# One table of moments for four engines, and a 16-bit split for the transposes

## The chip, the cores and the metric

The kernel runs on one core of one Trainium2 chip. The metric is the device time of one execution in microseconds (us), lower is better. In this text PE is the matrix engine (TensorE), DVE the vector engine, ACT the scalar engine (activations), POOL is GpSimd, and SP is the queue that issues all transfers. A trace of one execution is read through its views: the page, the stretches, the groups by line, the timeline of an engine, the waits.

## The reference, cut to what matters

```python
# q, k, v: (8 batches, 8 heads, 576 positions, 64)
scores = q @ k.T / sqrt(64)
mask = (rel >= 0) & (rel < 64)              # each query sees itself and the 63 keys before it
attn = softmax(where(mask, scores, -1e9))
x = (attn @ v) as (4608 tokens, 512)        # heads side by side
h = x @ w_in                                # w_in: (512, 2048), w_out: (2048, 512)
g = maximum(h, 0) + log1p(exp(-abs(h)))     # softplus
out = g @ w_out                             # (4608, 512)
```

## The kernel before

The 4608 tokens are cut into 12 blocks of 384 (`TB`). The attention of a block is done in four *pairs* of heads (128 of the 512 columns each), so there are 48 pairs. The FFN of a block has 16 *steps*, one for each 128 of the 2048 inner columns, so there are 192 steps.

A pair goes through stages. SP loads q, k and v. PE makes the scores (L216, 12 products, which the trace counts as 24 matmuls). DVE adds the mask and takes the row's extreme (L224, six times). ACT takes the exponential and its row sums (L235). DVE normalises (L243 to L245). The 384x128 attention weights have to be turned over. In the first two blocks (`by_pe`) PE does that (L253) and ACT copies both halves of the result to `pt` (L254). In the ten others the weights are scaled, ACT rounds them to 16 bits (L264, tile `nat`), DVE takes the rounded part away for a second 16-bit tile (L267), SP's transposing transfer turns both (L261, `tr`), and DVE adds them into `pt` (L271). Then PE multiplies with v (L285, called AV here), ACT rounds the result to the matrix engine's format (L290, first part of `x`), and DVE takes the remainder (L291, second part).

A step is an *up* group of 12 matmuls into one bank `ps_h` (L307), the softplus (ACT L311 to L313, DVE L315), the rounding of g and its remainder (L317 on ACT or DVE, L318 on DVE), and a *down* group of nine matmuls into three banks `ps_o` (L328). Weights, x and g are each held as a rounded part plus a remainder, and a product takes three matmuls. `ps_h` has two banks, g three buffers.

The weights come as 64-bit words in 16 *tiles*, one for each inner step (`load_w`). A tile is a 1 MB load, one ACT pass (L162), three DVE passes (L163 to L165), two rounding copies on ACT (L168) and two remainders on DVE (L169). Step f of any block needs tile f, so in the order of steps (four of block 0, sixteen of block 1, the other twelve of block 0, then block 2 and on) the twentieth step, which is number 19 when counted from 0, is the first to use tile 15. Steps are counted from 0 below.

The order of PE's instructions is the one in which the code is written out: `events` gives each stage a number by hand (`CONVERT`, `BASE`, `STG0`, `EARLY_UP` and so on) and sorts by it, and `MANUAL` keeps PE to that. The three other engines' orders (DVE, ACT, SP) are found by the framework's scheduler, which sees the same list.

Of the kernel before, what the change touches and what calls it, by code (L numbers as in the profile page):

```python
# [11 lines left out]
FP16 = mybir.dt.float16  # L12
# [31 lines left out]
def window_attention_softplus_ffn(  # L44
# [97 lines left out]
    def load_w(f):  # L142


        if f < NE + 4:
# [11 lines left out]
        for raw, w, m0, m1 in parts:
# [3 lines left out]
            wb = w.bitcast(U32)  # L161
            nc.scalar.activation(w, high.bitcast(F32), AF.Abs, scale=REBIAS)  # L162
            nc.vector.tensor_scalar(wb, wb, 3, None, ALU.logical_shift_left)  # L163
            nc.vector.scalar_tensor_tensor(wb, high, 0x80000000, wb, ALU.bitwise_and, ALU.bitwise_or)  # L164
            nc.vector.scalar_tensor_tensor(wb, low, 29, wb, ALU.logical_shift_right, ALU.bitwise_or)  # L165
            for m in range(m0, m1):
                hi, lo = [weight(m, i, f) for i in range(2)]
                nc.scalar.copy(hi, w[:, m - m0, :])  # L168
                nc.vector.tensor_tensor(lo, w[:, m - m0, :], hi.bitcast(F32), ALU.subtract)  # L169
# [5 lines left out]
    def attention(g, hp):  # L175
# [12 lines left out]
        q_in = ld.tile([P, TB], F32, name="q_in", bufs=2)  # L188
        k_in = ld.tile([P, CH + TB], F32, name="k_in", bufs=2)
# [7 lines left out]
        v_in = att.tile([P, 2 * NJ, P], F32, name="v_in", bufs=2)  # L197
# [8 lines left out]
        if g == 0:  # L206

            st = spare(FIRST[hp], [P, 2, NJ, P], F32, "st0")
        else:
            st = att.tile([P, 2, NJ, P], F32, name="st", bufs=2)  # L210
        mn = att.tile([P, 2, NJ], F32, name="mn", bufs=2)
        sm = att.tile([P, 2 * NJ], F32, name="sm", bufs=2)
# [7 lines left out]
        for j in range(NJ):  # L220
            t = (t0 + j * P) % S
            m = mask_at[0] if t == 0 else mask_at[1] if t + P > S else mask
            for hh in range(2):
                nc.vector.tensor_tensor_reduce(  # L224
                    st[:, hh, j, :], sps[hh][:, j * P : (j + 1) * P], m,
                    QSCALE, 3.0e38, ALU.add, ALU.min, mn[:, hh, j : j + 1],
                )
            if by_pe or j == NJ - 1:
                yield

        sv = st.rearrange("p h j c -> p (h j) c")
        for hh in range(2):
# [5 lines left out]
            if not by_pe:  # L238
                yield
        if by_pe:  # L240
            nc.vector.tensor_scalar(sm, sm, 1.0e-9, None, ALU.add)
        else:
            nc.vector.tensor_scalar(sm, sm, 1.0e-9, 1.0 / P_UNIT, ALU.add, ALU.mult)  # L243
        nc.vector.reciprocal(sm, sm)
        nc.vector.tensor_tensor(sv, sv, sm.unsqueeze(2).to_broadcast([P, 2 * NJ, P]), ALU.mult)  # L245
        if by_pe:

            yield
            pt = att.tile([P, 2, TB], F32, name="pt")
            for hh in range(2):  # L250
                pp = bank()
                for j in range(NJ):
                    tp(pp[:, j * P : (j + 1) * P], sv[:, hh * NJ + j, :], ident)  # L253
                nc.scalar.copy(pt[:, hh, :], pp[:, :TB])  # L254
        else:

            nat = att.tile([P, 2, 2 * NJ, P], FP16, name="nat")
# [6 lines left out]
            nc.scalar.copy(nat[:, 0, :, :], sv)  # L264
            turn(0)
            yield
            nc.vector.tensor_tensor(nat[:, 1, :, :], sv, nat[:, 0, :, :], ALU.subtract)  # L267
# [21 lines left out]
        unit = 1.0 if by_pe else 1.0 / P_UNIT  # L289
        nc.scalar.mul(x_t[0], av[:, :TB], unit)  # L290
        nc.vector.scalar_tensor_tensor(x_t[1], av[:, :TB], unit, x_t[0].bitcast(F32), ALU.mult, ALU.subtract)  # L291
# [7 lines left out]
    def ffn_up(g, f):  # L299
        x = xs[g]  # L300
        hps = ps_h.tile([P, 512], F32, name="ps_h")
        hv = hps[:, :TB]
        fs = slice(f * P, (f + 1) * P)
# [10 lines left out]
        gf = u  # L314
        nc.vector.scalar_tensor_tensor(gf, hv, 0.0, u, ALU.max, ALU.add)  # L315
        gt = [ff.tile([P, TB], F32R, name=f"g{i}", bufs=3) for i in range(2)]
        (nc.scalar.copy if g < 2 or f % 2 else nc.vector.tensor_copy)(gt[0], gf)  # L317
        nc.vector.tensor_tensor(gt[1], gf, gt[0].bitcast(F32), ALU.subtract)  # L318
# [110 lines left out]
```

## Time and profile before

| | |
|---|---|
| median of 3 runs | 969.87 us (968.57 to 971.11) |
| the profiled execution's own time | 974.21 us |
| its span, first to last instruction | 972.4 us |
| PE busy | 923.3 us, 95% |
| DVE busy | 539.0 us, 55% |
| ACT busy | 564.5 us, 58% |
| matmuls | 6384 |
| read from and written to memory | 56.62 MB and 10.22 MB |

The busy shares are means over very different parts: a beginning in which weights are made ready, and a long even stretch. The page cuts the span into 40 slices of 24.3 us and gives a digit for each (9 is 90% busy or more). A row of a timeline gives the start, the length, the engine, the line, output and inputs, how many instructions were merged, and in brackets the idle time ahead with what ended it. The length of a DVE or ACT row reaches a little into the next one, so what an instruction costs in a full queue is the distance between two starts.

### The profile page before, as it was taken

Reading aid. Unit: us, or ns where it says so; the run is one execution under the profiler, and the core shown is the slowest. Engines: PE = TensorE matmul, PEld = TensorE weight load, DVE = VectorE, ACT = ScalarE, POOL = GpSimd, SP = SyncE. Lnnn points to the kernel's source line nnn. Section 1 sums busy time; section 2 is a strip of 40 time slices with the busy share of each in tenths; the row PEclk is TensorE's granted clock in tenths of the full one; section 3 lists DMA queues with packets and bytes.
Section 4 is the critical chain, followed back from the end, with each engine's and each line's share of the span. In section 5 each row is a group of like instructions: output and inputs, shape, how many; then the busy total and the mean of one; then the engine's idle time right before and its main releaser. Section 6 shows DMA issues by size and latency. Waiting matters only on the chain.

```text
span 972.4 us, 16615 instructions
## 1 busy us (share of the span) xinstructions
PE 923.3 (95%) x6384; PEld 814.9 (84%) x6384; DVE 539.0 (55%) x1431; ACT 564.5 (58%) x1433; POOL 3.9 (0%) x23
## 2 busy tenths in 40 slices
PE   5458989999999999999999999999999999999998
PEld 4347978888888888888888888888888888889997
DVE  4897684646546545545555554554554555553332
ACT  5666676656555655655655555565565565554443
POOL 1000000000000000000000000000000000000000
PEclk9568989999999999999999999999999999999999
DMA  7764333513334212322321321322323332210000
GB/s 223 261 219 146 131 109 52 148 51 117 65 53 104 80 51 80 93 62 69 100 67 51 117 67 52 112 64 60 93 74 68 83 85 68 65 33 2 33 1 33
DMA packets 124047, 83.65 MB, mean 86 GB/s; under 512 B 67136, under 2 KB 116032, under 8 KB 122432
## 3 DMA queue, kind: packets, MB, share of 16 engines
q1 hardware_dynamic: 123968, 82.60, 30.3%
q8 instruction: 50, 0.82, 0.4%
q14 instruction: 29, 0.24, 0.1%
HBM read 56.62 MB, written 10.22 MB: 69 GB/s over the span
## 4 chain that ended last, share of the span: by engine, by line
PE 87%; DMA 6%; DVE 3%; ACT 3%; issue 0%; SPq 0%; ACTq 0%; DVEq 0%
PE ps_h L307 41%; PE ps_o L328 39%; PE ps_a L285 4%; DMA raws<-in_w_words_dram 4%; PE ps_a L216 3%; DMA raw<-in_w_words_dram 2%; ACT st L235 1%; ACT ws L162 1%; DVE w L169 1%; DVE ws L164 0%; DVE ws L165 0%; DMA part<-raw 0%; DVE st L245 0%; ACT wh L162 0%; DVE st L224 0%
## 5 line engine op out<-in xcount | busy, mean ns | idle before, releaser
L307 PE MATMUL ps_h<-x,w 128*128 128x384 f32 x2304 | 443.8, 341 | 3.4 <-DVE u L315 3.4
L328 PE MATMUL ps_o<-w,g 128*128 128x512 f32 x1728 | 433.5, 395 | 1.4 <-DVE g L318 1.4
L307 PEld LDWEIGHTS ps_h<-x,w 128*128 128x128 f32 x2304 | 409.1, 189 | 24.1 <-issue 6.9
L328 PEld LDWEIGHTS ps_o<-w,g 128*128 128x128 f32 x1728 | 322.2, 188 | 62.3 <-DVE g L318 2.0
L315 DVE SCALAR_TENSOR_TENSOR u<-ps_h,u 128x384 f32<-128x384 f32 x192 | 107.0, 557 | 253.4 <-ACT u L313 249.7
L311 ACT ACTIVATE u<-ps_h 128x384 f32<-128x384 f32 x192 | 93.5, 487 | 226.1 <-PE ps_h L307 226.1
L235 ACT ACTIVATE st<-st,mn 128x128 f32<-128x128 f32 x288 | 111.9, 391 | 67.1 <-DVE mn L224 67.1
L318 DVE TENSOR_TENSOR g<-u,g 128x384 fp32r<-128x384 f32 x192 | 106.6, 555 | 38.7 <-ACT g L317 33.8
L312 ACT ACTIVATE u<-u 128x384 f32<-128x384 f32 x192 | 100.9, 526 | 5.8
L313 ACT ACTIVATE u<-u 128x384 f32<-128x384 f32 x192 | 100.9, 525 | 5.7
L317 ACT CAST g<-u 128x384 fp32r<-128x384 f32 x112 | 57.4, 512 | 57.7 <-DVE u L315 56.6
L285 PEld LDWEIGHTS ps_a<-pt,v_in 128*64 128x64 f32 x1104 | 40.1, 146 | 34.1 <-issue 20.2
L224 DVE CUSTOM_DVE_ANT_0 st<-ps_a,mask 128x128 f32<-128x128 f32 x276 | 61.8, 286 | 9.6 <-PE ps_a L216 9.6
L285 PE MATMUL ps_a<-pt,v_in 128*64 128x64 f32 x1104 | 47.6, 236 | 16.8 <-ACT pt L254 11.3
L235 ACT ACTIVATION_READ_ACCUMULATOR st<-st,mn 128x1 f32 x288 | 54.0, 188 | 0.0
L271 DVE TENSOR_TENSOR pt<-tr 128x768 f32<-128x768 f16 x40 | 38.3, 958 | 22.8 <-PE ps_a L285 21.2
L216 PE MATMUL ps_a<-k_in,q_in 64*64 64x128 f32 x1104 | 44.8, 297 | 3.8 <-DMA k_in<-in_kT_dram 3.8
L245 DVE TENSOR_TENSOR st<-st,sm 128x768 f32<-128x768 f32 x48 | 46.0, 958 | 1.4
L216 PEld LDWEIGHTS ps_a<-k_in,q_in 64*64 64x64 f32 x1104 | 32.7, 144 | 8.6 <-POOL mask L135 3.8
L267 DVE TENSOR_TENSOR nat<-st,nat 128x768 f16<-128x768 f32 x40 | 38.1, 952 | 1.4 <-ACT nat L264 1.4
L243 DVE TENSOR_SCALAR sm<-sm 128x6 f32<-128x6 f32 x40 | 6.9, 172 | 54.4 <-ACT st L235 54.3
L264 ACT CAST nat<-st 128x768 f16<-128x768 f32 x40 | 33.3, 832 | 0.5 <-DVE st L245 0.5
(48 smaller groups left out, 295.6 us busy)
## 6 DMA issues: line engine op xcount, KB each, us to landing
v_in<-in_v_dram SPq DMA_DIRECT2D x44, 384.0 KB, 3.6
raws<-in_w_words_dram SPq DMA_DIRECT2D x12, 1024.0 KB, 7.2
k_in<-in_kT_dram SPq DMA_DIRECT2D x44, 224.0 KB, 4.0
q_in<-in_qT_dram SPq DMA_DIRECT2D x48, 192.0 KB, 3.7
out_dram<-raw SPq DMA_DIRECT2D x12, 512.0 KB, 3.0
raw<-in_w_words_dram SPq DMA_DIRECT2D x8, 512.0 KB, 3.9
out_dram<-raw SPq DMA_DIRECT2D x12, 256.0 KB, 4.3
v_in<-in_v_dram SPq DMA_DIRECT2D x4, 320.0 KB, 4.2
```

The costliest lines, as they stand in the source:

```text
L216: mm(sps[hh][halves[u], j * P : (j + 1) * P], q_in[heads[hh], a * CH : (a + 1) * CH], k_in[heads[hh], a * CH : (a + 2) * CH], start=True, ...
L224: nc.vector.tensor_tensor_reduce(st[:, hh, j, :], sps[hh][:, j * P : (j + 1) * P], m, QSCALE, 3.0e38, ALU.add, ALU.min, mn[:, hh, j : j + 1],)
L235: nc.scalar.activation(sv[:, i, :], sv[:, i, :], AF.Exp, bias=mn[:, hh, j : j + 1], scale=-1.0, accum_out=sm[:, i : i + 1])
L285: mm(av[heads[hh], cs], v_in[:, a, heads[hh]], pt[:, hh, cs], start=(a == 0), stop=(a == 2 * NJ - 1), skip_group_check=True,)
L307: mm(hv, weight(0, a, f)[:, c * P : (c + 1) * P], x[b][c], start=(i_mm == 0), stop=(i_mm == 3 * NC - 1))
L311: nc.scalar.activation(u, hv, AF.Abs)
L312: nc.scalar.activation(u, u, AF.Exp, scale=-1.0)
L313: nc.scalar.activation(u, u, AF.Ln, bias=1.0)
L315: nc.vector.scalar_tensor_tensor(gf, hv, 0.0, u, ALU.max, ALU.add)
L317: (nc.scalar.copy if g < 2 or f % 2 else nc.vector.tensor_copy)(gt[0], gf)
L318: nc.vector.tensor_tensor(gt[1], gf, gt[0].bitcast(F32), ALU.subtract)
L328: mm(ops[g][j], gt[a][:, js], weight(1, b, f), start=(first and i == 0), stop=(last and i == 2),)
```

## The change

All stages, those of the pairs, of the tiles and of the steps, get a moment from one table. `put` hands a stage's offsets out, the list is sorted by moment, and all four engines (PE, DVE, ACT and SP) are kept to the order in which the code is then written out. Stages are cut finer for that: a conversion has seven, an up step five, a pair thirteen or fifteen.

- All eight pairs of the first two blocks stand ahead of the first step; the four steps of block 0 follow, with block 1 behind them.
- The weight tiles 8 to 15 each get a buffer of their own, which also serves as a landing place (`RAW`) or a working place (`WORDS`) for earlier tiles. One tile's load is in halves (tile 15), where before there were four (12 to 15).
- q, k, v and the small tiles of a pair have three buffers instead of two, `pt` two instead of one.
- In the first two blocks DVE copies the second half of the turned weights (L255), which ACT did before.
- In the other ten, the 32-bit weights are cut into their low and high 16 bits as integers: ACT copies the low halves (L268), DVE the high ones (L271), the transfer turns both, and ACT (L275) and DVE (L277) put them together in `pt`. No scaling and no rounding is left in it; the factor `P_UNIT` is gone.

```diff
-DOWN = 5.5
-CONVERT = (-64.5, -44.5, -14, -2, 0, 1, 2, 4, 6, 8, 10, 12, 14, 16, 18, 20)
-BASE = (-80, -40, 24)
-EARLY_UP, EARLY_DOWN = {0: -16.5, 1: -6.4}, {0: -6.5, 1: 5.5}
-MANUAL = {mybir.EngineType.PE}
...
+TILES = (1.6, 27.5, 24.4, 17.7, 43.2, 45.0, 53.8, 65.9, 63.2, 76.8, 78.5, 82.6, 90.5, 98.0, 99.3, 108.9)
+EARLY_AT = (43.0, 46.1, 52.0, 48.8, 58.1, 57.8, 66.8, 71.4, 72.9, 79.8, 82.2, 85.7)
+MANUAL = {mybir.EngineType.PE, mybir.EngineType.DVE, mybir.EngineType.Activation, mybir.EngineType.SP}
...
+    RAW = (8, 9, 10, 11) * 2 + (9, 10, 11, 12, 13, 14, 15, 0)
+    WORDS = (12, 13, 14, 15) * 3 + (0, 0, 0, 0)
...
-        q_in = ld.tile([P, TB], F32, name="q_in", bufs=2)
-        k_in = ld.tile([P, CH + TB], F32, name="k_in", bufs=2)
+        q_in = ld.tile([P, TB], F32, name="q_in", bufs=3)
+        k_in = ld.tile([P, CH + TB], F32, name="k_in", bufs=3)
...
-            for hh in range(2):
-                pp = bank()
-                for j in range(NJ):
-                    tp(pp[:, j * P : (j + 1) * P], sv[:, hh * NJ + j, :], ident)
-                nc.scalar.copy(pt[:, hh, :], pp[:, :TB])
+            yield
+            nc.scalar.copy(pt[:, 0, :], pps[0][:, :TB])
+            yield
+            nc.vector.tensor_copy(pt[:, 1, :], pps[1][:, :TB])
...
-            nc.scalar.copy(nat[:, 0, :, :], sv)
-            turn(0)
-            yield
-            nc.vector.tensor_tensor(nat[:, 1, :, :], sv, nat[:, 0, :, :], ALU.subtract)
-            turn(1)
-            yield
-            pt = att.tile([P, 2, TB], F32, name="pt")
-            nc.vector.tensor_tensor(
-                pt, *[tr[:, s, :, :].rearrange("p (h j) q -> p h (j q)", h=2) for s in range(2)], ALU.add
-            )
+            nc.scalar.copy(nat[:, 0, :], cut[:, 0, :])
+            yield
+            turn(0)
+            nc.vector.tensor_copy(nat[:, 1, :], cut[:, 1, :])
+            yield
+            turn(1)
+            yield
+            nc.scalar.copy(joint[:, 0, :], tr[:, 0, :, :].rearrange("p i q -> p (i q)"))
+            yield
+            nc.vector.tensor_copy(joint[:, 1, :], tr[:, 1, :, :].rearrange("p i q -> p (i q)"))
...
+    def put(stages, at, offsets):
+        for offset in offsets:
+            events.append((at + offset, lambda: next(stages, None)))
...
+        at = max(at, EARLY_AT[n] if n < len(EARLY_AT) else FIRST_STEP + SLOT * n)
+        put(ffn_up(g, f), at, UP)
+        events.append((at + AHEAD, lambda step=steps[n]: ffn_down(*step)))
```

Three places show what the change moves. The first is PE around its first step: `ps_h` rows are the step's up group, `ident` rows turn the weights of a pair, `pt,v_in` rows are its AV, `k_in,q_in` rows the scores of the next pair. Before:

```order
L216 MATMUL ps_a<-k_in,q_in 64x128 x12
L253 MATMUL ps_a<-ident,st 128x128 x6
L285 MATMUL ps_a<-pt,v_in 64x64 x12
L216 MATMUL ps_a<-k_in,q_in 64x128 x12
L307 MATMUL ps_h<-x_0_0_230,w_85 128x384
...
L307 MATMUL ps_h<-x_3_0_443,w_86 128x384
L253 MATMUL ps_a<-ident,st 128x128 x6
L285 MATMUL ps_a<-pt,v_in 64x64 x12
L216 MATMUL ps_a<-k_in,q_in 64x128 x12
L328 MATMUL ps_o_646<-w_87,g_569 128x512
```

And PE at the same place after the change:

```order
L220 MATMUL ps_a<-k_in,q_in 64x128 x12
L289 MATMUL ps_o_531<-pt,v_in 64x64 x12
L289 MATMUL ps_a<-pt,v_in 64x64 x12
L251 MATMUL ps_a<-ident,st 128x128 x12
L289 MATMUL ps_a<-pt,v_in 64x64 x12
L251 MATMUL ps_a<-ident,st 128x128 x6
L289 MATMUL ps_a<-pt,v_in 64x64 x24
L313 MATMUL ps_h<-x_0_0_314,w_85 128x384
```

The first steps stood between the pairs of block 1; now all of these pairs' work, up to the last AV, stands ahead of the first step, and four up groups follow one another.

The second place is DVE where the conversions of tiles and the first steps meet (`ws` and `w` rows are a tile, `u` and `g` rows a step). Before:

```order
L318 TENSOR_TENSOR g_677<-u,g_676 128x384
L315 SCALAR_TENSOR_TENSOR u<-ps_h,u 128x384
L169 TENSOR_TENSOR w_839<-ws,w_838 128x512
L169 TENSOR_TENSOR w_843<-ws,w_842 128x512
L318 TENSOR_TENSOR g_791<-u,g_790 128x384
L291 SCALAR_TENSOR_TENSOR x_3_1_815<-ps_a,x_3_1_814 128x384
L163 TENSOR_SCALAR ws<-ws 128x1024
L164 SCALAR_TENSOR_TENSOR ws<-raws,ws 128x1024
L165 SCALAR_TENSOR_TENSOR ws<-raws,ws 128x1024
L315 SCALAR_TENSOR_TENSOR u<-ps_h,u 128x384
```

DVE from the first step on, after the change:

```order
L322 SCALAR_TENSOR_TENSOR u<-ps_h,u 128x384
L167 TENSOR_SCALAR ws<-ws 128x1024
L168 SCALAR_TENSOR_TENSOR ws<-raws,ws 128x1024
L169 SCALAR_TENSOR_TENSOR ws<-raws,ws 128x1024
L322 SCALAR_TENSOR_TENSOR u<-ps_h,u 128x384
L327 TENSOR_TENSOR g_744<-u,g_743 128x384
L167 TENSOR_SCALAR ws<-ws 128x1024
L168 SCALAR_TENSOR_TENSOR ws<-raws,ws 128x1024
L169 SCALAR_TENSOR_TENSOR ws<-raws,ws 128x1024
L327 TENSOR_TENSOR g_784<-u,g_783 128x384
```

Before, the first steps meet the last full-size conversions; now they meet the fifth and the sixth, so conversions and steps run side by side for eleven tiles, and the three passes of a tile always stand together.

The third place is ACT in the even stretch, around one pair (`st` rows are exponentials, `nat` and `pt<-tr` the 16-bit halves, `x` the result of AV, the rest are steps). Before:

```order
L290 ACTIVATE x_2_0_5698<-ps_a 128x384
L235 ACTIVATE st,sm<-st,mn 128x128 x6
L311 ACTIVATE u<-ps_h 128x384
L312 ACTIVATE u<-u 128x384
L313 ACTIVATE u<-u 128x384
L264 CAST nat<-st 128x768
L311 ACTIVATE u<-ps_h 128x384
```

And ACT after the change:

```order
L268 COPY nat<-st 128x768
L294 CAST x_0_0_3799<-ps_a 128x384
L318 ACTIVATE u<-ps_h 128x384
L319 ACTIVATE u<-u 128x384
L320 ACTIVATE u<-u 128x384
L275 COPY pt<-tr 128x768
L238 ACTIVATE st,sm<-st,mn 128x128 x3
```

The six exponentials are cut into two groups of three, and a copy out of `tr` (L275) is new on ACT, one step behind the copy into `nat`.

More of the change, by code (lines that the diff above doesn't have):

```diff
@@ L165, in load_w @@
             nc.vector.scalar_tensor_tensor(wb, low, 29, wb, ALU.logical_shift_right, ALU.bitwise_or)
[L166 to L169, printed above, removed]
+        yield
+        for m in range(2):
+            hi, lo = [weight(m, i, f) for i in range(2)]
+            nc.scalar.copy(hi, w[:, m, :])
+            yield
+            nc.vector.tensor_tensor(lo, w[:, m, :], hi.bitcast(F32), ALU.subtract)
+            written.add((m, f))
+            yield
     xs = {}
@@ L195, in attention @@
         yield
-        v_in = att.tile([P, 2 * NJ, P], F32, name="v_in", bufs=2)
+        v_in = att.tile([P, 2 * NJ, P], F32, name="v_in", bufs=3)
         a0 = 1 if t0 == 0 else 0
@@ L204, in attention @@
         yield
[L206 to L212, printed above, removed]
+        st = att.tile([P, 2, NJ, P], F32, name="st", bufs=3)
+        mn = att.tile([P, 2, NJ], F32, name="mn", bufs=3)
+        sm = att.tile([P, 2 * NJ], F32, name="sm", bufs=3)
         sps = [bank() for _ in heads]
@@ L237, in attention @@
                 )
-            if not by_pe:
-                yield
[L240 to L243, printed above, removed]
+            yield
+        nc.vector.tensor_scalar(sm, sm, 1.0e-9, None, ALU.add)
         nc.vector.reciprocal(sm, sm)
         nc.vector.tensor_tensor(sv, sv, sm.unsqueeze(2).to_broadcast([P, 2 * NJ, P]), ALU.mult)
+        yield
+        pt = att.tile([P, 2, TB], F32, name="pt", bufs=2)
@@ L260, in turn @@
+            yield
+            nc.vector.tensor_copy(pt[:, 1, :], pps[1][:, :TB])
+        else:
+            nat = att.tile([P, 2, 2 * NJ * P], U16, name="nat")
+            tr = att.tile([P, 2, 2 * NJ, P], U16, name="tr")
+            cut, joint = [
+                t.bitcast(U16).rearrange("p (n two) -> p two n", two=2)
+                for t in (sv.rearrange("p i k -> p (i k)"), pt.rearrange("p h q -> p (h q)"))
+            ]
             def turn(s):
-                nc.sync.dma_start(tr[:, s, :, :], nat[:, s, :, :].rearrange("p i k -> p (i k)"), transpose=True)
+                nc.sync.dma_start(tr[:, s, :, :], nat[:, s, :], transpose=True)
+            nc.scalar.copy(nat[:, 0, :], cut[:, 0, :])
@@ L300, in ffn_up @@
         x = xs[g]
+        assert {(0, f)} | {("x", g, hp) for hp in range(NP)} <= written
         hps = ps_h.tile([P, 512], F32, name="ps_h")
         hv = hps[:, :TB]
-        fs = slice(f * P, (f + 1) * P)
         i_mm = 0
@@ L308, in ffn_up @@
                 i_mm += 1
+        yield
         u = ff.tile([P, TB], F32, name="u")
```

122 lines of the change are left out of this document (61 added, 61 removed).

## The prediction

> **What bounds the kernel now.** I read the page's 40 slices first, then the busy time in hand-cut stretches, then PE's timeline through the beginning, then DVE's for what its work costs, and last the even stretch. The page:
>
> ```profile
> span 972.4 us, 16615 instructions
> ...
> PE   5458989999999999999999999999999999999998
> ...
> PEclk9568989999999999999999999999999999999999
> ```
>
> From about the seventh slice on PE is full and at full clock. The stretches give time, then busy us with the number of instructions of PE, weight loads, DVE, ACT and POOL, then the granted clock, the DMA share and GB/s:
>
> ```profile
> 5.54:20.00 14.46, 7.93 (x86) 6.17 (x86) 8.09 (x38) 7.90 (x30) 0.51 (x3) 0.99 0.75 235
> 20.00:40.00 20.00, 8.98 (x105) 7.46 (x106) 16.74 (x51) 14.28 (x42) 0.20 (x1) 0.50 0.84 282
> 40.00:60.00 20.00, 9.97 (x107) 7.52 (x106) 18.15 (x39) 13.13 (x38) 0.00 (x0) 0.50 0.63 222
> 60.00:80.00 20.00, 11.96 (x92) 9.62 (x91) 18.32 (x49) 13.66 (x40) 0.00 (x0) 0.90 0.62 218
> 80.00:100.00 20.00, 18.24 (x120) 16.70 (x121) 16.18 (x24) 14.84 (x30) 0.00 (x0) 0.83 0.29 93
> 100.00:120.00 20.00, 20.00 (x101) 18.01 (x100) 12.51 (x24) 13.02 (x26) 0.00 (x0) 1.00 0.43 145
> 120.00:139.90 19.90, 17.00 (x104) 14.45 (x102) 17.34 (x42) 14.78 (x38) 0.00 (x0) 0.98 0.39 128
> 165.87:968.00 802.13, 802.13 (x5503) 711.24 (x5499) 418.59 (x1138) 456.60 (x1157) 0.00 (x0) 1.00 0.26 69
> ```
>
> Two regimes. From 165.87 to 968 PE is busy for all of 802.13 us, and only less PE work could shorten that. From 20 to 80 DVE is busy 53.2 of 60 us and PE 30.9: the beginning is bound by the vector engine, which makes weights ready and masks scores. PE's timeline (L307: an up group is x12, two are x24; L328: a down group is x9; L216 and L285: x24 are one pair's scores or AV):
>
> ```profile
> 59.23 1.01 PE L307 MATMUL ps_h<-x,w 128*128 128x384 f32 x2
> 91.53 4.47 PE L307 MATMUL ps_h<-x,w 128*128 128x384 f32 x24
> 140.36 4.21 PE L307 MATMUL ps_h<-x,w 128*128 128x384 f32 x12 [3.36 <-DVE u L315]
> 144.37 3.00 PE L328 MATMUL ps_o<-w,g 128*128 128x512 f32 x9
> 162.87 2.25 PE L328 MATMUL ps_o<-w,g 128*128 128x512 f32 x9
> 165.05 0.89 PE L216 MATMUL ps_a<-k_in,q_in 64*64 64x128 f32 x24
> 165.87 2.35 PE L307 MATMUL ps_h<-x,w 128*128 128x384 f32 x12
> ```
>
> Step 0 starts at 59.23 and steps 3 and 4 at 91.53. From there PE works at its own pace but for one hole ahead of 140.36, though tile 15 is ready only near 139.9. The up group at 165.87 is the twentieth, step 19, the first that needs tile 15. From it to the end are 972.4 - 165.87 = 806.5 us. By both orders, 17 down groups and three scores of block 2 stand ahead of it, before and after, and the groups behind it are the same. So the new span is T19, the start of step 19, plus 806.5, as long as PE stays full behind it.
>
> **The change, part by part.** *DVE's work up to tile 15.* No step 19 without the rounded part and the remainder of tile 15's first half. Before, DVE is busy 8.09 + 16.74 + 18.15 + 18.32 + 16.18 + 12.51 + 17.34 = 107.3 us up to there. What single things cost there (DVE timeline; distances between starts count):
>
> ```profile
> 22.59 0.17 DVE L241 TENSOR_SCALAR sm<-sm 128x6 f32<-128x6 f32 x1 [0.67 <-ACT st L235]
> ...
> 23.90 1.29 DVE L169 TENSOR_TENSOR w<-ws,w 128x512 fp32r<-128x512 f32 x2
> ...
> 63.71 0.28 DVE L224 CUSTOM_DVE_ANT_0 st<-ps_a,mask 128x128 f32<-128x128 f32 x1
> ...
> 64.97 1.29 DVE L169 TENSOR_TENSOR w<-ws,w 128x512 fp32r<-128x512 f32 x2
> ...
> 93.50 0.69 DVE L163 TENSOR_SCALAR ws<-ws 128x1024 uint32<-128x1024 uint32 x1 [0.62 <-ACT ws L162]
> 94.23 1.23 DVE L164 SCALAR_TENSOR_TENSOR ws<-raws,ws 128x1024 uint32<-128x1024 uint32 x1
> 95.50 1.23 DVE L165 SCALAR_TENSOR_TENSOR ws<-raws,ws 128x1024 uint32<-128x1024 uint32 x1
> 96.64 0.55 DVE L315 SCALAR_TENSOR_TENSOR u<-ps_h,u 128x384 f32<-128x384 f32 x1
> 97.63 1.29 DVE L169 TENSOR_TENSOR w<-ws,w 128x512 fp32r<-128x512 f32 x2 [0.44 <-ACT w L168]
> 98.84 0.55 DVE L315 SCALAR_TENSOR_TENSOR u<-ps_h,u 128x384 f32<-128x384 f32 x1
> 99.31 1.22 DVE L318 TENSOR_TENSOR g<-u,g 128x384 fp32r<-128x384 f32 x2
> ```
>
> A normalisation is 23.90 - 22.59 = 1.31 us, a pair's six masks 64.97 - 63.71 = 1.26, a tile's passes 96.64 - 93.50 = 3.14 and its remainders 98.84 - 97.63 = 1.21, a step's operation 0.47. By the orders the work up to the same point differs so: one more pair's masks (+1.3), the eight copies L255 (below, +3.8), six more L322 and five more L327 (11 x 0.47 = +5.2), one remainder less (-0.6). That is 107.3 + 9.7 = 117.0.
>
> L255 reads 384 columns from PSUM; no such DVE copy is in the trace. Groups by line (mean ns of one, after the busy us):
>
> ```profile
> L291 DVE SCALAR_TENSOR_TENSOR x<-ps_a,x 128x384 fp32r<-128x384 f32 x46 | 25.3, 551 | 1.2 <-ACT x L290 1.1
> L347 DVE COPY raw<-ps_o 128x512 f32<-128x512 f32 x24 | 16.5, 687 | 18.3 <-PE ps_o L328 18.3
> L317 DVE CAST g<-u 128x384 fp32r<-128x384 f32 x80 | 28.8, 360 | 5.7
> L267 DVE TENSOR_TENSOR nat<-st,nat 128x768 f16<-128x768 f32 x40 | 38.1, 952 | 1.4 <-ACT nat L264 1.4
> L264 ACT CAST nat<-st 128x768 f16<-128x768 f32 x40 | 33.3, 832 | 0.5 <-DVE st L245 0.5
> ```
>
> It lies between 360 (384 columns, not from PSUM) and 687 (512 from PSUM). I take 551, the row with its own size and memory, 0.47 in a queue; the eight are 3.8, with ends of 2.9 and 5.5.
>
> *DVE's order.* The three passes of a tile, and those of a normalisation, now follow one another without filler. A dependent one starts 0.04 behind its forerunner's end (94.23 against 93.50 + 0.69), an independent one 0.09 ahead of it (96.64 against 95.50 + 1.23). Two such joints in 16 tiles and 9 normalisations are 50 x 0.13 = 6.5 at most; since part was so before, 5.
>
> *Waits.* DVE starts at 5.54. From there to 20 it was idle 6.4 us, between dependent stages of single pairs; with three pairs' scores ahead I take 4. From 20 to 100 it was idle 80 - 69.4 = 10.6, or 13%. A fixed order over all engines can wait more (nothing fills in) or less (it was laid for this); I take 10% of the 111 us of work that are then left, 11 us. Bounds: 4% and 18%, or 4 and 20 us.
>
> T19 by DVE: 5.5 + 117.0 + 5 + 4 + 11 = 142.5.
>
> *PE.* The last AV ahead of step 0 needs DVE's eighth L255. Ahead of that stand eight masks and normalisations (8 x 2.57 = 20.6), eight copies (3.8), five remainders of x (2.4), two tiles and the passes of a third (2 x 4.35 + 3.14 = 11.8): 38.6. With 5.5 of start, 4 and 10% of waits that is 52, and with the AV step 0 starts at 53 to 54, only some 5 earlier than now. What follows is the gain: 19 up and 17 down groups of 2.1 us (162.87 to 165.05 is one, with 0.1 of it for the next) and three scores of 0.8 to 0.9 are 78, so PE could reach step 19 at 132. DVE ends last, by 10 us.
>
> *ACT and SP.* ACT was busy 85% of what DVE was up to 139.9; it loses the eight copies and gains six steps' four passes, so it stays behind DVE. On SP the load of tile 3 now stands behind the v load of the eighth pair, which waits for the fifth pair's AV, near 40 by the same kind of sum. The landing takes 7.2:
>
> ```profile
> raws<-in_w_words_dram SPq DMA_DIRECT2D x12, 1024.0 KB, 7.2
> ```
>
> So tile 3 is there at 47 to 48, and DVE wants it behind the eighth L255, at 52. That hides it; each us over 4 would go into T19 in full.
>
> *The even stretch.* A period (AV, scores, four steps) on PE, what ACT waits for two steps behind the pair, and the transposing transfer:
>
> ```profile
> 515.58 0.92 PE L285 MATMUL ps_a<-pt,v_in 128*64 128x64 f32 x24
> ...
> 517.24 2.35 PE L307 MATMUL ps_h<-x,w 128*128 128x384 f32 x12
> ...
> 534.20 0.92 PE L285 MATMUL ps_a<-pt,v_in 128*64 128x64 f32 x24
> ```
>
> ```profile
> 513.60 0.49 ACT L311 ACTIVATE u<-ps_h 128x384 f32<-128x384 f32 x1 [2.58 <-PE ps_h L307]
> ```
>
> ```profile
> DMA to landing us min/median/max: 2.5/2.5/4.8
> ```
>
> PE's 18.62 us a period hold the same groups in the same neighbourhood after the change (AV and scores adjacent in 40 pairs, before and after), so nothing is won or lost there. The 16-bit copies: DVE has two 768-column operations a pair as before, ACT two for one. Near 832 and 952 ns (the rows with their size; half or double, as no row shows an integer copy with gaps), ACT goes from 456.6 to 456.6 + 40 x 0.83 = 490 of 802. The cover is that ACT waits 2.58 us for PE in one step; without cover it would cost 0.83 x 40 = 33. L275 waits for a transfer that lands 2.5 after its issue, and ACT has a step (4.2) in between. I cost all this at nothing.
>
> Sum: span 142.5 + 806.5 = 949.0, 23.4 less. The profiled execution would take 974.2 - 23.4 = 950.8, and the median, which is 2.5 below the old span, 946.5.
>
> **The rivals.** *PE ends last in the beginning.* If DVE waits next to nothing behind 20 us, T19 is 132 by either sum and the time 936. For it: DVE came to 91% in 40 to 80. Against: there its order was chosen with fillers.
>
> *The beginning waits more.* DVE waits 20 to 25% of 111 (22 to 28 us), or PE loses its clock: ups come in twos in the new order, so DVE's near 5.8 us a step (a tile's 4.35, two operations of 0.47, joints and waits) against PE's 4.2 leave PE holes of about 3.2 between twos. The hole of 3.36 us at 140.36 made one up 4.21 instead of 2.1 and the down 3.00 instead of 2.2, 2.9 together. Eight such are 23 on PE's 132, T19 = 155. Either way the time is near 958, at most 963. The Trainium skill's page "TensorE: Matmul & The Clock Gate" (section "Why this matters for your kernels") says that holes over about 3 us between bursts cost the full clock; by that rule this rival would be the outcome if the twos hold. This trace agrees at 140.36.
>
> *Slower: ACT's queue in the even stretch.* L275 waits for its transfer while the next step's L318 stands behind it; when that is later than PE's spare time, PE waits in each of 40 periods. At the full 0.83 us it costs 33, the time 980. It decides from 23.4 / 40 = 0.6 us a period. Against: 2.58 us of spare time and landings of at most 4.8.
>
> *No change.* The fixed order waits so much that T19 is near 165 again, DVE waiting 34 instead of 11: 967 to 972.
>
> **How the numbers follow.** Forecast 0.66 (its own range by 4 and 20 us of waits and the ends of L255: 938 to 957), PE last 0.08, more waits 0.13, slower 0.07, no change 0.06. A measurement here can tell about 0.3%, 3 us. Faster: 0.66 + 0.08 + 0.13 = 0.87; within: 0.06; slower: 0.07. The range 935 to 963 leaves out the last two and little else.
>
> **What would show it.** Right: step 0 near 53, step 19 at 138 to 151 with 806 us behind it, DVE over 85% busy from 20 to 140, PE without holes behind step 19, the period at 18.6. Wrong: step 19 past 160 (the beginning), holes on PE behind it with ACT's L318 late and L275 waiting for DMA (the even stretch), clock digits under 9 between 60 and 140 (the gate). Most likely to break the forecast is the share of waiting, which no row shows for the new order.

## The result, and the profile after

| | before | after |
|---|---|---|
| median of the compared runs | 969.22 us (967.82 to 971.11) | 937.62 us (936.81 to 938.36) |
| ratio, 95% interval | | 0.9673, 0.9652 to 0.9693 |
| profiled execution, and its span | 974.21 us, 972.4 us | 938.34 us, 936.6 us |
| start of step 0 and of step 19 | 59.23, 165.87 us | 49.46, 133.19 us |
| from step 19 to the end | 806.5 us | 803.4 us |
| DVE from 5.54 to step 19: busy, idle | 119.7, 40.6 us | 117.8, 9.9 us |

The kernel became faster by 31.6 us at the median. The spans of the profiled pair differ by 35.8, because the profiled execution of before lay 5.0 above its median and that of after 0.7. Of these 35.8, 32.7 lie ahead of step 19 and 3.1 behind it. That long execution of before seems to have lost its 5 us in the beginning: the old kernel with the new 16-bit arithmetic alone (below) has a span of 967.2, reaches step 19 at 160.66, and has the same 806.5 behind it.

The page of after, with the span, PE's busy tenths in 40 slices, DVE's, and PE's granted clock:

```profile
span 936.6 us, 16685 instructions
...
PE   5689999999999999999999999999999999999998
...
DVE  5989995445455445545555455445445544543332
...
PEclk7899999999999999999999999999999999999999
```

PE is full from the fourth slice on instead of from the seventh, and its clock digit is 9 from the third on, though the stretch from 40 to 60 below still reads 0.74. The same stretches as before, cut at the new step 19 (time, then busy us of PE, weight loads, DVE, ACT, POOL, then clock, DMA share, GB/s):

```profile
5.54:20.00 14.46, 7.98 (x94) 6.16 (x96) 11.80 (x51) 8.89 (x39) 0.16 (x1) 0.76 0.80 250
20.00:40.00 20.00, 13.85 (x236) 10.79 (x234) 17.84 (x83) 16.81 (x67) 0.20 (x1) 0.91 0.76 247
40.00:60.00 20.00, 15.47 (x120) 13.08 (x120) 19.28 (x29) 12.95 (x28) 0.00 (x0) 0.74 0.54 210
60.00:80.00 20.00, 19.47 (x96) 17.14 (x96) 17.73 (x27) 16.87 (x31) 0.00 (x0) 1.00 0.44 154
80.00:100.00 20.00, 20.00 (x102) 18.19 (x101) 19.46 (x28) 16.45 (x30) 0.00 (x0) 1.00 0.46 170
100.00:120.00 20.00, 19.89 (x138) 17.03 (x138) 18.69 (x36) 15.90 (x34) 0.00 (x0) 1.00 0.94 320
120.00:133.19 13.19, 13.19 (x86) 11.50 (x85) 12.95 (x34) 10.40 (x29) 0.00 (x0) 1.00 0.16 37
133.19:932.23 799.04, 799.02 (x5500) 711.78 (x5499) 388.65 (x1148) 483.56 (x1210) 0.00 (x0) 1.00 0.29 70
```

Two things are to be seen. DVE is busy 82 to 98% of every stretch up to step 19, where before it was busy 56% of the first (8.09 of 14.46) and fell to 63% in a later one (12.51 of 20, from 100 to 120). Of its idle time before, some 35 of the 40.6 us were waits for a result of ACT; after, 6 of the 9.9. And PE runs beside it: from 60 on it is full while DVE is still converting tiles. Before, in the stretch from 60 to 80, DVE was as busy and PE had 11.96 of 20.

PE's timeline at the start of the steps and at step 19 (L251 turns weights, L289 is AV, L313 an up group, L339 a down group):

```profile
35.85 1.00 PE L251 MATMUL ps_a<-ident,st 128*128 128x128 f32 x6
40.75 1.74 PE L251 MATMUL ps_a<-ident,st 128*128 128x128 f32 x6 [3.91 <-DVE st L244]
43.30 1.54 PE L289 MATMUL ps_a<-pt,v_in 128*64 128x64 f32 x24 [0.81 <-ACT pt L253]
...
48.62 0.92 PE L289 MATMUL ps_a<-pt,v_in 128*64 128x64 f32 x24 [0.95 <-DVE pt L255]
49.46 2.38 PE L313 MATMUL ps_h<-x,w 128*128 128x384 f32 x12
52.85 0.61 PE L313 MATMUL ps_h<-x,w 128*128 128x384 f32 x2 [1.00 <-ACT w L173]
54.47 5.53 PE L313 MATMUL ps_h<-x,w 128*128 128x384 f32 x22 [1.01 <-DVE w L175]
...
131.00 2.35 PE L339 MATMUL ps_o<-w,g 128*128 128x512 f32 x9
133.19 2.38 PE L313 MATMUL ps_h<-x,w 128*128 128x384 f32 x12
```

And DVE at the same end (L175 at 132.83 is the first remainder of tile 15):

```profile
131.75 0.69 DVE L169 SCALAR_TENSOR_TENSOR w<-raw,w 128x512 uint32<-128x512 uint32 x1
132.36 0.55 DVE L322 SCALAR_TENSOR_TENSOR u<-ps_h,u 128x384 f32<-128x384 f32 x1
132.83 0.68 DVE L175 TENSOR_TENSOR w<-w,w 128x512 fp32r<-128x512 f32 x1
133.50 0.56 DVE L327 TENSOR_TENSOR g<-u,g 128x384 fp32r<-128x384 f32 x1
```

Step 19 starts with no bracket, so PE did not stand waiting for tile 15. That first remainder ends at 133.51, when the group has been running for 0.32 us; only the third of its matmuls needs it. The two engines end together.

The new operations, as groups by line (mean ns of one):

```profile
L275 ACT COPY pt<-tr 128x768 uint16<-128x768 uint16 x40 | 42.2, 1055 | 1.2 <-DMA tr<-nat 1.1
L268 ACT COPY nat<-st 128x768 uint16<-128x768 uint16 x40 | 32.6, 816 | 0.0
L277 DVE COPY pt<-tr 128x768 uint16<-128x768 uint16 x40 | 24.1, 602 | 0.0
L271 DVE COPY nat<-st 128x768 uint16<-128x768 uint16 x40 | 22.2, 554 | 0.0
L255 DVE COPY pt<-ps_a 128x384 f32<-128x384 f32 x6 | 3.3, 551 | 0.9 <-PE ps_a L251 0.9
```

### The profile page after: what moved, and what is told of

It reads as the page before. It is cut to its first block, busy times and chain, and to the rows that moved or that the text cites. A ratio compares the mean times of both kernels' runs of the same rounds, so it can differ in the third digit from the quotient of the medians.

```text
span 936.6 us, 16685 instructions
## 1 busy us (share of the span) xinstructions
PE 910.4 (97%) x6384; PEld 806.9 (86%) x6384; DVE 507.1 (54%) x1430; ACT 583.1 (62%) x1462; POOL 3.9 (0%) x23
## 3 DMA queue, kind: packets, MB, share of 16 engines
q1 hardware_dynamic: 123536, 82.60, 32.7%
## 4 chain that ended last, share of the span: by engine, by line
PE 92%; DVE 4%; ACT 1%; DMA 1%; issue 0%; POOL 0%; SPq 0%; POOLq 0%
PE ps_o L339 42%; PE ps_h L313 42%; PE ps_a L289 4%; PE ps_a L220 4%; DMA raws<-in_w_words_dram 1%; DVE w L175 1%; DVE ws L168 1%; DVE st L228 1%; ACT ws L161 0%; DVE st L244 0%; DVE ws L169 0%; DVE x L296 0%; DVE ws L167 0%; DVE pt L255 0%; ACT st L238 0%
## 5 line engine op out<-in xcount | busy, mean ns | idle before, releaser
L313 PE MATMUL ps_h<-x,w 128*128 128x384 f32 x2304 | 436.0, 338 | 2.5 <-DVE w L175 1.0
L339 PE MATMUL ps_o<-w,g 128*128 128x512 f32 x1728 | 433.4, 395 | 0.1
L313 PEld LDWEIGHTS ps_h<-x,w 128*128 128x128 f32 x2304 | 409.4, 188 | 19.7 <-DVE w L175 1.5
L339 PEld LDWEIGHTS ps_o<-w,g 128*128 128x128 f32 x1728 | 318.7, 188 | 66.0 <-issue 6.4
L318 ACT ACTIVATE u<-ps_h 128x384 f32<-128x384 f32 x192 | 94.3, 491 | 291.3 <-PE ps_h L313 288.6
L322 DVE SCALAR_TENSOR_TENSOR u<-ps_h,u 128x384 f32<-128x384 f32 x192 | 106.8, 557 | 276.2 <-ACT u L320 276.1
L320 ACT ACTIVATE u<-u 128x384 f32<-128x384 f32 x192 | 100.8, 525 | 6.1
L289 PEld LDWEIGHTS ps_a<-pt,v_in 128*64 128x64 f32 x1104 | 37.5, 143 | 13.4 <-issue 10.5
L289 PE MATMUL ps_a<-pt,v_in 128*64 128x64 f32 x1104 | 44.0, 231 | 1.8 <-DVE pt L255 1.0
L275 ACT COPY pt<-tr 128x768 uint16<-128x768 uint16 x40 | 42.2, 1055 | 1.2 <-DMA tr<-nat 1.1
L296 DVE TENSOR_TENSOR x<-ps_a,x 128x384 fp32r<-128x384 f32 x46 | 25.6, 556 | 20.9 <-ACT x L294 20.9
L268 ACT COPY nat<-st 128x768 uint16<-128x768 uint16 x40 | 32.6, 816 | 0.0
L325 DVE CAST g<-u 128x384 fp32r<-128x384 f32 x80 | 28.2, 353 | 1.7
```

What stands on the lines that cost most here:

```text
L289: mm(av[heads[hh], cs], v_in[:, a, heads[hh]], pt[:, hh, cs], start=(a == 0), stop=(a == 2 * NJ - 1), skip_group_check=True,)
L313: mm(hv, weight(0, a, f)[:, c * P : (c + 1) * P], x[b][c], start=(i_mm == 0), stop=(i_mm == 3 * NC - 1))
L318: nc.scalar.activation(u, hv, AF.Abs)
L320: nc.scalar.activation(u, u, AF.Ln, bias=1.0)
L322: nc.vector.scalar_tensor_tensor(u, hv, 0.0, u, ALU.max, ALU.add)
L339: mm(ops[g][j], gt[a][:, js], weight(1, b, f), start=(first and i == 0), stop=(last and i == 2),)
```

## The experiments

All are compared with the kernel before in runs on the same chip: 970.08 us for the first four, 970.57 for the second four, 970.03 for the last four (969.22 in the result above). Those that start from the changed kernel say so.

### Which part of the change gains: the order or the arithmetic

**PE alone in the written order** (from the changed kernel):

```diff
-MANUAL = {mybir.EngineType.PE, mybir.EngineType.DVE, mybir.EngineType.Activation, mybir.EngineType.SP}
+MANUAL = {mybir.EngineType.PE}
```

> The change with only PE kept to the written order; DVE, ACT and SP are ordered by the framework's scheduler again. Theory A (the gain is the shorter beginning, and it needs all four engines in one order, because DVE is full there and must do first what PE needs first): step 19 starts at 140 to 160 instead of 133, time 945 to 965. Rival B (PE's new order and the buffers alone make the gain): step 19 within 3 us of 133, time 935 to 941.

966.75 us (965.67 to 968.22), ratio 0.9965 [0.9952, 0.9977]. Rival B falls: nearly all of the gain needs the other queues to be kept to the table. Theory A's range was missed by 2 us on the slow side, and its step 19 (140 to 160) by 1.4. The stretches and the first up group of this kernel:

```profile
20.00:40.00 20.00, 11.62 (x156) 9.12 (x156) 20.00 (x52) 15.49 (x43) 0.20 (x1) 0.77 0.97 349
40.00:60.00 20.00, 10.17 (x114) 7.21 (x108) 20.00 (x52) 12.11 (x37) 0.00 (x0) 0.55 0.49 160
60.00:80.00 20.00, 12.13 (x105) 10.41 (x105) 19.85 (x43) 12.46 (x31) 0.00 (x0) 0.66 0.63 207
```

```profile
76.53 5.40 PE L313 MATMUL ps_h<-x,w 128*128 128x384 f32 x24
```

DVE is as good as full from 20 to 80, and yet step 0 comes 27 us later than with all four orders. A full engine is no proof of good progress here: it did tiles, for which nobody waited yet, ahead of the pairs, for which PE waited. By 36 us the last pass of four tiles (L169) stands in its timeline, in the change of one. Then, once PE's steps run, DVE waits for them: it is busy only 6.97 of the 20 us from 120 to 140 and idle 37.3 in all up to step 19 (161.41). No run kept the order and took the new buffers back, so how much of the order's gain needs the buffers stays open; all parts of the change but the order of DVE, ACT and SP together gave 3 us.

**The old 16-bit arithmetic in the new places** (from the changed kernel: rounding to `nat`, remainder, sum, and the factor `P_UNIT`), and **the integer halves alone** (from the kernel before, where the same lines are exchanged the other way round):

```diff
-            nc.scalar.copy(nat[:, 0, :], cut[:, 0, :])
+            nc.scalar.copy(nat[:, 0, :, :], sv)
...
-            nc.vector.tensor_copy(nat[:, 1, :], cut[:, 1, :])
+            nc.vector.tensor_tensor(nat[:, 1, :, :], sv, nat[:, 0, :, :], ALU.subtract)
...
-            nc.scalar.copy(joint[:, 0, :], tr[:, 0, :, :].rearrange("p i q -> p (i q)"))
...
-            nc.vector.tensor_copy(joint[:, 1, :], tr[:, 1, :, :].rearrange("p i q -> p (i q)"))
+            nc.vector.tensor_tensor(
+                pt, *[tr[:, s, :, :].rearrange("p (h j) q -> p h (j q)", h=2) for s in range(2)], ALU.add
+            )
```

> The change with the old turning arithmetic put back in its new places (scaled weights rounded to 16 bits by ACT, remainder by DVE, sum by DVE). Theory A: the even stretch is PE's, DVE is covered there; time 936 to 940, the stretch behind step 19 as long as in the change within 1 us. Rival C (the integer halves give PE back some us, as the profile after is 3.1 us shorter behind step 19 than before): time 940 to 942, the stretch 2 to 4 us longer.

> The kernel before with only the integer 16-bit halves: two copies into the halves, two out of them, no scaling. Theory A: nothing, 967 to 972. Rival C: 2 to 4 us faster, 965 to 967. Rival D (the extra ACT copy in a queue that the scheduler fills costs PE time): 975 or more.

The old arithmetic in the new places takes 936.98 us (936.68 to 937.53), ratio 0.966 [0.9631, 0.969]; the integer halves alone 971.33 (968.43 to 973.65), ratio 1.0012 [0.9996, 1.0029]. Neither differs from its parent, and theory A was met both times. The halves are worth nothing in time, though behind step 19 they take 30 us of work from DVE (419.16 with the old arithmetic in the new places, 388.65 in the change) and put 35 on ACT (448.91 to 483.56): there PE is the bound.

**One engine beside PE in the written order**, for each of the three others (from the changed kernel; the line of `MANUAL` again):

```diff
+MANUAL = {mybir.EngineType.PE, mybir.EngineType.DVE}
...
+MANUAL = {mybir.EngineType.PE, mybir.EngineType.SP}
...
+MANUAL = {mybir.EngineType.PE, mybir.EngineType.Activation}
```

> The changed kernel with only PE and DVE kept to the written order; ACT and SP are left to the scheduler. With PE alone kept to it, DVE is busy 59.85 of the 60 us from 20 to 80, yet step 0 starts only at 76.5: DVE did the tiles ahead of the pairs. Theory A (DVE's order is what gains): step 19 at 132 to 140, 937 to 945 us. Rival H (the order of loads on SP, with ACT's, is what gains, DVE only follows): step 19 past 150, 955 to 967 us.

> Only PE and SP kept to the written order; DVE and ACT are left to the scheduler. Theory A: DVE still takes tiles ahead of pairs where their loads are there, step 19 past 150, 955 to 967 us. Rival H (loads in the right order lead DVE to the right order): step 19 at 132 to 142, 937 to 947 us.

> Only PE and ACT kept to the written order. ACT's first pass of a tile is what DVE's passes need, so ACT's order could lead DVE to the right one. Theory A: step 19 past 150, 955 to 967 us. Rival I (ACT's order is enough): step 19 at 132 to 145, 937 to 950 us.

| kept to the table | median, us | ratio, 95% interval | step 0 | step 19 | DVE idle from 5.54 to step 19 |
|---|---|---|---|---|---|
| PE | 966.75 | 0.9965 [0.9952, 0.9977] | 76.53 | 161.41 | 37.3 |
| PE, DVE | 951.48 | 0.9806 [0.9789, 0.9822] | 54.45 | 145.92 | 22.2 |
| PE, SP | 949.19 | 0.9783 [0.9768, 0.9797] | 50.72 | 140.67 | 14.7 |
| PE, ACT | 948.53 | 0.9780 [0.9765, 0.9794] | 49.57 | 141.59 | 19.3 |
| all four (the change) | 937.62 | 0.9673 [0.9652, 0.9693] | 49.46 | 133.19 | 9.9 |

Theory A falls in all three: it had put everything on DVE and expected 937 to 945 for that queue and 955 or more for the two others. Rival H falls too: the run of DVE was 3.5 us faster than it said and that of SP 2 us slower. Rival I's ranges were met (948.53, step 19 at 141.59), but ACT's order is not enough either, as 11 us are missing. Any one queue gives some 15 to 18 us over PE alone, and the other 11 to 14 came only with all of them; two of the three together were not tried. The first part is step 0, which comes at 50 to 54 as soon as any one queue stops the tiles from running ahead, be it the load, ACT's first pass or DVE's own: at 36 us each of these three kernels has done the last pass of one tile, as the change has. The rest lies mostly between step 0 and step 19, where these three take 90 to 92 us and the change 83.7; PE's idle time there is 8.0 to 8.8 us against 2.65. With DVE's queue alone step 0 is also 5 us late, and behind step 19 the three lose another 0.8 to 2.8. Two rows for each show the waits, for DVE, SP and ACT in this order, near step 1 or 3 and at step 19:

```profile
67.62 3.67 PE L313 MATMUL ps_h<-x,w 128*128 128x384 f32 x12 [3.94 <-DVE u L322]
...
145.92 2.27 PE L313 MATMUL ps_h<-x,w 128*128 128x384 f32 x12
```

```profile
64.16 2.38 PE L313 MATMUL ps_h<-x,w 128*128 128x384 f32 x12 [3.02 <-DVE u L322]
...
140.67 2.27 PE L313 MATMUL ps_h<-x,w 128*128 128x384 f32 x12
```

```profile
55.52 9.21 PE L313 MATMUL ps_h<-x,w 128*128 128x384 f32 x36 [3.59 <-ACT w L173]
...
141.59 0.62 PE L313 MATMUL ps_h<-x,w 128*128 128x384 f32 x2 [1.31 <-ACT w L173]
```

### What sets step 19 now

**Less work on DVE** (from the changed kernel; the second combining pass of each tile is left out, so the weights lack their last bits):

```diff
-            nc.vector.scalar_tensor_tensor(wb, low, 29, wb, ALU.logical_shift_right, ALU.bitwise_or)
```

> The change without the third DVE pass of each tile (L169, which puts the words' low bits in; the weights lose their last bits): 16 x 1.2 = 19 us less DVE work in the beginning, PE's work unchanged. Theory A (DVE and PE reach step 19 together at 133): PE's sum stays, step 0 comes 2 to 4 us earlier, step 19 at 128 to 131, time 932 to 936. Rival E (DVE alone ends last, PE follows it): step 19 at 114 to 120, time 918 to 925.

933.2 us (932.42 to 934.35), ratio 0.9621 [0.9595, 0.9646]: theory A's range of time is met, though step 0 came only 1.3 us earlier and not 2 to 4, and rival E is far off. DVE's busy time up to step 19 falls by 15.6 us (117.75 to 102.14; the expectation reckoned with 19), step 19 by 5.4:

```profile
48.13 4.66 PE L312 MATMUL ps_h<-x,w 128*128 128x384 f32 x24
...
127.79 2.27 PE L312 MATMUL ps_h<-x,w 128*128 128x384 f32 x12
```

From step 0 to step 19 PE now takes 79.7 us instead of 83.7, and DVE is idle 20.1 us up to there. Of the work that was taken from DVE two thirds came back as waiting. That settles that DVE alone no longer binds: PE is idle for 0.72 us between the two steps, so its own sum (78 by the prediction) is nearly reached.

**Single edits near that tie** (from the changed kernel). L255 on ACT; tile 1 converted earlier, in exchange with tile 3; both:

```diff
-            nc.vector.tensor_copy(pt[:, 1, :], pps[1][:, :TB])
+            nc.scalar.copy(pt[:, 1, :], pps[1][:, :TB])
...
-TILES = (1.6, 27.5, 24.4, 17.7, 43.2, 45.0, 53.8, 65.9, 63.2, 76.8, 78.5, 82.6, 90.5, 98.0, 99.3, 108.9)
+TILES = (1.6, 17.7, 24.4, 27.5, 43.2, 45.0, 53.8, 65.9, 63.2, 76.8, 78.5, 82.6, 90.5, 98.0, 99.3, 108.9)
```

> The changed kernel with the copy of the second half of pt (L255) back on ACT, so DVE has 8 x 0.55 = 4.4 us less work ahead of step 19, and ACT that much more. Theory A (PE's own sum, from step 0 on, and DVE's end together; what is taken off one of them alone gains little): step 0 moves by at most 1 us, step 19 at 131 to 133, 936 to 938 us. Rival F (DVE's work alone still sets step 19; the lighter DVE of the earlier run gained what DVE's last part gave): step 19 some 4 us earlier, 933 to 934.5 us.

> The changed kernel with two numbers of the table exchanged: tile 1 is converted at 17.7 and tile 3 at 27.5, so that the first four tiles come in the order in which steps use them but for tile 2. The order of kinds on every engine is the same. Now step 1 waits 1.00 us for ACT's and 1.01 us for DVE's part of tile 1. Theory A: these two waits go, DVE's work stays, so step 19 is 0 to 2 us earlier, 935.5 to 937.6 us. Rival F (DVE alone): no change, 937 to 938.2 us. Either way step 1 must follow step 0 without idle time, unless a load is late.

> Both edits at once: tile 1 earlier and L255 on ACT, so that PE and DVE both are relieved. Theory A (they end together): more than the two edits alone, step 19 at 129 to 131.5, 933.5 to 936 us. Rival F (DVE alone): the same as L255 on ACT alone, 933 to 934.5 us for both. Rival G (ACT, which takes eight copies more, then ends last): 938 us or more.

L255 on ACT: 935.66 us (935.47 to 936.55), ratio 0.9646 [0.9629, 0.9663], step 19 at 131.39. Tile 1 earlier: 937.39 (937.21 to 938.99), 0.9666 [0.9649, 0.9684], step 19 at 132.10. Both: 935.84 (934.46 to 937.75), 0.9648 [0.9628, 0.9667], step 19 at 129.29. These intervals overlap with that of the change, so no gain over it is proven. Nor do they decide between the theories. Rival F's 933 to 934.5 is not met, and theory A's times are met but for 0.3 us in the first; but theory A wanted more from both edits than from each, and both together took no less than L255 on ACT alone. The step 19 of the single edits proves nothing either. The kernel with the old arithmetic has the change's beginning, but for the form of some operations on `x` and on block 2's first pairs (DVE's work up to step 19 is 117.5 us), and its profile has step 19 at 131.49, 1.7 us ahead of the change's. Its waits of 1.03 and 1.00 us at step 1 left the next 22 matmuls at 4.09 us (granted clock 1.00 from 50 to 60), where in the change's profile 1.00 and 1.01 stand ahead of 5.53 (granted clock 0.54 and 0.61 from 54 to 58). So a difference of up to 1.7 us in step 19 between two profiles can be the clock and not the edit. Only that of both edits lies further off, in the fastest of its four runs. What becomes of a removed wait is to be seen in the kernel with tile 1 earlier:

```profile
49.43 4.43 PE L313 MATMUL ps_h<-x,w 128*128 128x384 f32 x24
55.97 2.39 PE L313 MATMUL ps_h<-x,w 128*128 128x384 f32 x12 [2.11 <-DVE u L322]
59.59 2.35 PE L313 MATMUL ps_h<-x,w 128*128 128x384 f32 x12 [1.23 <-DVE u L322]
```

Step 1 follows step 0 at once, and the 2 us come back as the wait of step 2 and of step 3 for DVE's operation on `u`. Step 3 starts 10.16 us behind step 0; in the kernel with the old arithmetic, where step 1 has both waits and the clock is full as well, it is 10.17 (48.85 to 59.02).

**The first twelve steps later or earlier in the table.** 3 us later (from the changed kernel), and 2 us earlier (from the one with both edits):

```diff
-EARLY_AT = (43.0, 46.1, 52.0, 48.8, 58.1, 57.8, 66.8, 71.4, 72.9, 79.8, 82.2, 85.7)
+EARLY_AT = (46.0, 49.1, 55.0, 51.8, 61.1, 60.8, 69.8, 74.4, 75.9, 82.8, 85.2, 88.7)
...
+EARLY_AT = (41.0, 44.1, 50.0, 46.8, 56.1, 55.8, 64.8, 69.4, 70.9, 77.8, 80.2, 83.7)
```

> The changed kernel with the twelve moments of the first steps (EARLY_AT) 3 us later in the table. All pairs stand ahead of the first step in either case, so step 0 itself hardly moves; DVE gets tiles ahead of steps a little earlier, and down groups and step operations move back in the order. Theory A (PE's sum binds as much as DVE's): step 19 is 0 to 3 us later, 938 to 941 us. Rival F (DVE alone, by its tiles): tile 15 is ready earlier, step 19 one or two us earlier, 935.5 to 937 us.

> Tile 1 earlier and L255 on ACT, as before, and the twelve moments of the first steps 2 us earlier in the table (3 us later cost 9 us). In the kernel with both edits steps 2 and 3 still wait 1.05 and 1.25 us for DVE's operation on u (L322). Theory A (steps on DVE ahead of tiles is the right side to err on, while tile 15 has spare time): step 19 at 127 to 129.3, 932 to 935.8 us. Rival J (the table stands at its best, tiles now come too late): step 19 1 to 9 us later, 937 to 945 us.

Later: 946.72 us (946.31 to 947.88), ratio 0.976 [0.9743, 0.9778]. Theory A had the direction and was far off in size (9 us for 3); rival F had the wrong sign. Earlier: 940.65 us (939.96 to 943.01), 0.9702 [0.9688, 0.9717], 4.8 slower than its parent, as rival J said. In the later table PE meets these waits:

```profile
53.16 0.62 PE L313 MATMUL ps_h<-x,w 128*128 128x384 f32 x2 [1.03 <-ACT w L173]
...
63.52 2.38 PE L313 MATMUL ps_h<-x,w 128*128 128x384 f32 x12 [3.09 <-DVE u L322]
...
141.28 2.27 PE L313 MATMUL ps_h<-x,w 128*128 128x384 f32 x12
```

Step 0 is at 49.77, so PE loses its 8 us behind it, 6.3 of them waiting for DVE's operation on `u` (0.5 in the change). DVE's work is nearly the same (119.4 us), and its idle time up to step 19 is 16.4 us instead of 9.9. On the other side, with steps 2 us earlier, it is 15.0 (9.5 in its parent), with 4.2 of it for ACT's part of a step (L322 behind L320; 1.3 in its parent). Both shifts lose. Smaller ones, and shifts of single steps, were not tried, so how near to its best the table stands is not known.

## Why the prediction was right, and where not

*The structure held.* The time moved with T19 and little else. From step 19 on PE is busy 799.02 of 799.04 us. In the twelve experiments the rest behind step 19 stayed between 803 and 807.

*DVE's work held.* It was put at 117.0 us and measured 117.75. L255 took 548 to 558 ns in its eight places, the size of the row it was priced by. One small count was off: five L322 more and not six.

*The step that was mis-sized is DVE's waits.* The prediction had 5 us of joints, 4 us of waits ahead of 20 and 11 behind, 20 in all. The trace has 9.9: 2.66 up to 20 (14.46 less 11.80), and 7.2 behind, with 1.8 in all that are joints (52 gaps of 0.03 us behind DVE's own forerunner):

```profile
20.00:133.19 113.19, 101.87 (x773) 87.74 (x772) 105.95 (x232) 89.38 (x213) 0.20 (x1) 0.94 0.57 199
```

That is 113.19 less 105.95, 6% of the stretch, joints included, where 10% of the work and the joints were taken. All three terms were too large. The 10.1 us too many here and 0.75 too few in the work make the 9.3 by which T19 came earlier than 142.5. The share was taken from the old kernel's 13%, and the runs show why no row of it could give a better one: nearly the same work in a table 3 us off waits 16.4 us and has step 19 at 141.28, 1.2 us from the predicted 142.5.

*"DVE ends last, by 10 us" failed.* Step 0 came at 49.46, not at 53 to 54, and PE took 83.7 us from it to step 19 instead of 78: 2.65 idle, and 81.08 busy, of which some 1.4 are the 22 matmuls at a lower clock (5.53 against 4.09). So PE reaches step 19 at 133.2 (132 was written) and DVE ends there too. The prediction's first rival, "PE ends last", which gave 132 and 936, is what the trace is nearest to; its chance, 0.08, was too small. The argument against it was that DVE's 91% from 40 to 80 had been reached with fillers. In the new order DVE comes to 94% from 20 on without a free choice. So the measured 937.62 lies just below the forecast's own range of 938 to 957, and inside 935 to 963 because that range took in this rival. That the gain lies ahead of step 19 was foreseen; that it is a third larger was not.

*The sum to the median.* The prediction took the new median 2.5 below the new span, as the old one stood to the old span. It stands 1.0 above it. The old distance was that of one long execution and no property of the kernel, so these 3.5 us are chance, and by chance they brought the forecast nearer. Together: 9.3 earlier at T19, 3.1 less behind it, 3.5 more from span to median, which is the 8.9 between 946.5 and 937.6.

*The 3.1 behind step 19* were costed at nothing. They go with PE's order: with PE alone in the table the rest is 803.2, with the integer halves alone 806.5, with the old arithmetic in the new places 803.4. (Where PE and one more queue are kept to the table it is 804.2 to 806.2; with ACT, the longest, most of the excess is the group of step 19 itself, which waits 1.05 us once more and then takes 3.51 us for ten matmuls.) The distance of AVs shows it, over 32 periods before and 31 after:

```profile
273.43 0.92 PE L285 MATMUL ps_a<-pt,v_in 128*64 128x64 f32 x24
...
869.59 0.92 PE L285 MATMUL ps_a<-pt,v_in 128*64 128x64 f32 x24
```

```profile
260.61 0.92 PE L289 MATMUL ps_a<-pt,v_in 128*64 128x64 f32 x24
...
835.91 0.92 PE L289 MATMUL ps_a<-pt,v_in 128*64 128x64 f32 x24
```

A period is 18.63 before and 18.56 after. After the scores now stands a down group, where an up group stood before; why groups of one size then take 0.02 to 0.03 us less each was not tried and stays open.

*What was hidden stayed hidden.* The load that stands behind the eighth pair's v load is the fourth, that of tile 1; the prediction called it tile 3, which is second in the table. It was there when ACT's first pass of that tile came, at 46.14, without a wait. L275 waited 1.1 us in all 40 periods, against the rival's 23.4, although it is dearer than priced (1055 against 832 ns):

```profile
L318 ACT ACTIVATE u<-ps_h 128x384 f32<-128x384 f32 x192 | 94.3, 491 | 291.3 <-PE ps_h L313 288.6
```

ACT still waits for PE 1.5 us a step (288.6 over 192), which is the cover that was named.

*The clock.* The rival of more waits did not come: the clock reads 1.00 from 60 on. Between PE's first matmul and step 19 one hole of over 3 us was left, the 3.91 ahead of 40.75, and behind it six transposes took 1.74 instead of 1.00 and an AV 1.54 instead of 0.92, at a granted clock of 0.50 from 42 to 46. The Trainium skill's page "TensorE: Matmul & The Clock Gate" (section "Why this matters for your kernels") warns of holes over about 3 us between bursts of matmuls. This hole agrees; the 3.09 us hole of the table with later steps, at the edge of that figure, left the next up group at 2.38. The rule was applied to holes that the prediction only supposed, between up groups in twos: those were 0.17 and 0.36 us in the trace.

## What to carry to other kernels

Where several in-order queues feed one bound engine, look at whose results a busy engine makes, not at how busy it is: DVE at 100% on work that nobody waited for put off step 0 by 27 us. Fixing one more queue got rid of most of that, whichever it was, while the last 11 to 14 us came only with one order on all of them, and a shift of the first steps by 2 or 3 us took 5 to 9 us back. Once two engines end together, price an edit at a fraction of what it removes: 15.6 us less DVE work gave 5.4, and two removed waits came back one and two steps later. And before a difference of 1 or 2 us between two profiles is put down to an edit, compare the granted clock of both.

## What the runs showed of the hardware beyond that

- A 16-bit copy of 768 columns on DVE took 554 to 602 ns, not the 952 that the two-source operation of that size took before. The Trainium skill's page "VectorE: DVE Perf Modes" (section "What auto-detection actually checks") says that an operation with a single source may take a mode of double rate when source and destination both lie in SBUF, the on-chip working memory, and their shapes fit. The trace agrees, and the prediction had priced by the row of a two-source operation. No run here varied the number of sources alone.
- On ACT the copy with the gaps on the writing side took longer: 1055 ns into `pt` (L275) against 816 out of `st` (L268). No run changed the side alone.
- The length of a hole did not tell whether PE lost its clock behind it. In the table with later steps the 22 matmuls of steps 1 and 2 behind two waits of 1.03 and 1.00 us took 5.65 (granted clock 0.50 from 56 to 58), and in the change 5.53 behind 1.00 and 1.01; behind 1.03 and 1.00 they took 4.22 with PE and DVE in the written order and 4.09 with the old arithmetic (granted clock 1.00 in both). Behind a single hole of 2.00 (PE and SP) the clock fell to 0.50, behind one of 2.11 (tile 1 earlier) it did not; six transposes behind one of 3.10 (tile 1 earlier) took 1.75, and the up group behind the one of 3.09 took its full-clock 2.38. What decides is not shown. Later steps; PE and DVE; the old arithmetic; PE and SP:

```profile
54.78 5.65 PE L313 MATMUL ps_h<-x,w 128*128 128x384 f32 x22 [1.00 <-DVE w L175]
```

```profile
59.45 4.22 PE L313 MATMUL ps_h<-x,w 128*128 128x384 f32 x22 [1.00 <-DVE w L175]
```

```profile
53.85 4.09 PE L315 MATMUL ps_h<-x,w 128*128 128x384 f32 x22 [1.00 <-DVE w L176]
```

```profile
55.48 5.66 PE L313 MATMUL ps_h<-x,w 128*128 128x384 f32 x22 [2.00 <-DVE w L175]
```
